# The small early load of wqkv entries: 64 entries over all 640 rows in place of 16 over the first 128

## The chip, the cores and the metric

The kernel runs on one core of one Trainium2 chip. The metric is the device time of one execution in microseconds (us), taken as the median over runs. Before the change it is 274.14 us, the median of 6 runs from 273.8 to 274.5.

## What is computed

The inputs are bf16: x is 2048 x 640 (S x D), wqkv 640 x 1920, wo 640 x 640, w_gate and w_up 640 x 1728, w_down 1728 x 640, gate_w 640 long. With H = 32 heads of 20:

```
def _A_ref(x, wqkv, wo):
    qkv = (x @ wqkv).reshape(B, S, 3, H, Dh) ...            # q, k, v
    phi = lambda t: jnp.where(t > 0, t + 1, jnp.exp(t)) + 1e-6
    pq, pk = phi(q), phi(k)
    kv = einsum("bhsd,bhse->bhde", pk, v);  z = sum of pk over s
    o = (pq @ kv) / (pq . z + 1e-6)
    return o @ wo                                           # heads joined again
def _B_ref(x, w_gate, w_up, w_down):
    return (gelu(x @ w_gate) * (x @ w_up)) @ w_down
g = sigmoid((A_x * gate_w).sum(-1, keepdims=True))
out = g * _A_ref(A_x, A_wqkv, A_wo) + (1 - g) * _B_ref(A_x, B_w_gate, B_w_up, B_w_down)
```

The columns 0 to 639 of wqkv give q, 640 to 1279 give k, 1280 to 1919 give v. One row of wqkv is 3840 bytes in DRAM.

## The kernel before

The program is a plan: `P.op(engine, function, reads, writes)` appends an instruction to its engine's list, and works out from the named reads and writes which semaphores it waits for. At the end the lists are emitted in the order in which they were written. Each engine (TensorE as PE, VectorE as DVE, ScalarE as ACT, GpSimd as POOL, SyncE as SP) runs its own list in order. A load given to "sp" or "act" is issued by that engine's queue, and each has its own semaphore. The 16 DMA engines of the core serve both queues.

The work goes in stages: K and Q projections with phi (a start for tiles 0 and 1, then `KQ(i)` at L540 for tiles 2 to 15), the product of pk and x (`MM`, L597), the feed-forward matmuls (`G`, L701) with the attention's small products between them, and the output tiles (`O_tile`, L865).

The change is in the start. There the loads are written out by hand:

- ACT's queue: first the early load of L357 into `touch`, 16 columns at the end of the SBUF pool, which nothing reads and whose semaphore nobody waits for. Then x tile 1, wk chunks 2 and 4, gate_w, and wq rows 256 to 639 (`load_wq(2, KC, "act")`).
- SP's queue: x tile 0, wk chunks 0, 1 and 3, wq rows 0 to 255 (`load_wq(0, 2)`). Then the DMA transposes of x tiles 2 to 15 (L375), the first of which waits for wk chunk 4.

All but the early load and the transposes are issued at L340. A chunk k is 128 rows of wqkv, `A_wqkv[k * 128:(k + 1) * 128, ...]`, one row per SBUF partition; `load_wk` takes columns 640 to 1279 of it and `load_wq` columns 0 to 639.

PE's list at the start: matmuls on constants (`warm`, L419), transposes of x tile 0 (`T`, L433), more `warm`, the first K matmul of tile 0, the transposes of tile 1, then the K matmuls (`KM`, L453 and L454) of both tiles over chunks 0, 1, 3, then 2 and 4, with the small `gate_col` (L498) between. Then come the Q matmuls (`QM`, L468 and L469), tile 0 and tile 1 in turn over chunks 0, 1, 2, then 3 and 4. The first four need wq chunks 0 and 1, which come by SP's load; the fifth is the first to need the load on ACT's queue. After these `KQ(2)` needs the transposed x tile 2.

The early load reads four numbers of a row, from column 640 on. Before the change these are rows 0, 8, 16, ..., 120, one to each of partitions 0 to 15.

Of the kernel before, what the change touches and what calls it, by code (L numbers as in the profile page):

```python
# [161 lines left out]
def bass_gated_mix__linear_attn_block__geglu_ffn__prompt_kernel(  # L162
# [63 lines left out]
    with (  # L226
# [8 lines left out]
        with contextlib.ExitStack() as stack:  # L235
            dma_sems = [stack.enter_context(nc.semaphore("s_in%d" % i)) for i in range(n_dma_in)]

            P = _Plan(["pe", "act", "dve", "pool", "sp"])
# [9 lines left out]
            def new_dma_key():  # L248
                k = "in%d" % dma_next[0]
                dma_next[0] += 1  # L250
                return k

            def v16(o, n):
                return pool[:, o:o + n]
# [46 lines left out]
            touch = v16(O_TOUCH, 16)  # L301
# [49 lines left out]
            def load_wq(k0, k1, eng="sp"):  # L351
# [2 lines left out]
                       r_wq[k0:k1], eng=eng)  # L354


            P.op("act", lambda e: e.dma_start(touch[0:16, 0:4], A_wqkv[0:128:8, 640:644]),  # L357
                 writes=[P.res("touch")], dma=new_dma_key())
            load_x(0)
            load_wk(0)  # L360
# [569 lines left out]
```

## Time and profile before

| | before |
|---|---|
| median of 6 runs | 274.14 us (273.8 to 274.5) |
| profiled execution, its own time | 274.5 us |
| its span, first to last instruction | 273.3 us |
| mean granted TensorE clock | 1.000 |
| busy, PE / DVE / ACT / POOL | 269.6 / 141.9 / 75.9 / 30.0 us |
| moved by DMA | 23.61 MB, mean 86 GB/s |

How to read the lines below: times are us from the span's start unless marked ns. A group's line has source line, engine, operation, output and input, and a count. In the chain of work each line is a start, a duration, and an engine or transfer; "SPq" is SP issuing a DMA, "issue" is time in which the engine waited for nothing that the profile shows. In the waits, "A <- B: total, times, longest" says that A stood still until B. In the view of one source line, the three durations in ns are the shortest, the median and the longest, and then first and last start. In the list of DMA issues the last number is the median us from issue to landing.

### The profile page before, as it was taken

The numbers are of one execution on the slowest core, as the hardware profiler recorded it, in microseconds if no ns is written. First come the engines' busy times: TensorE is split into PE (matmuls) and PEld (weight loads), VectorE is DVE, ScalarE is ACT, GpSimd is POOL, SyncE is SP. The second block draws the span as 40 slices with busy tenths as digits, with TensorE's granted clock in tenths as the row PEclk, the third lists the DMA queues.
The fourth block names the chain that finished last, engine by engine and source line by source line (L and its number), as shares of the span: only waits on it lengthen the run. The fifth ranks groups of instructions, "written<-read, shape, count | busy, mean of one in ns | idle before, by whom it ended". The sixth has DMA issues, their size and how long they took to land.

```text
span 273.3 us, 3449 instructions
## 1 busy us (share of the span) xinstructions
PE 269.6 (99%) x1369; PEld 128.5 (47%) x1369; DVE 141.9 (52%) x251; ACT 75.9 (28%) x132; POOL 30.0 (11%) x28
## 2 busy tenths in 40 slices
PE   8899999999999999999999999999999999999997
PEld 4455555544445444444444444444444444444444
DVE  2588989998234324999999999634210000000200
ACT  2355555300421454223222223224011121121021
POOL 5000000002240001242433422000000000000000
PEclk9999999999999999999999999999999999999999
DMA  6976999600300011522221211263031110110211
GB/s 210 190 103 124 317 401 388 147 3 9 67 19 2 22 49 51 181 46 48 27 48 24 48 41 35 60 216 108 5 77 38 41 38 19 38 41 19 58 58 41
DMA packets 42160, 23.61 MB, mean 86 GB/s; under 512 B 31519, under 2 KB 40735, under 8 KB 42015
## 3 DMA queue, kind: packets, MB, share of 16 engines
q1 hardware_dynamic: 41269, 22.40, 30.5%
q10 hardware_dynamic: 874, 0.98, 1.0%
q8 instruction: 11, 0.18, 0.3%
q14 instruction: 6, 0.05, 0.1%
HBM read 13.83 MB, written 2.63 MB: 60 GB/s over the span
## 4 chain that ended last, share of the span: by engine, by line
PE 96%; DMA 2%; SPq 1%; issue 0%; DVE 0%
PE ps L701 41%; PE ps L865 23%; PE ps L540 14%; PE ps L597 6%; PE ps L844 4%; DMA pool<-in_A_wqkv_dram 2%; PE ps L812 2%; PE ps L679 2%; PE ps L600 1%; PE ps L468 1%; PE ps L825 1%; SPq L340 1%; PE ps L722 1%; PE ps L740 0%; PE ps L469 0%; PE ps L607 0%
## 5 line engine op out<-in xcount | busy, mean ns | idle before, releaser
L701 PE MATMUL ps<-pool 128*128 128x512 bf16 x520 | 113.7, 379 | 0.0
L701 PEld LDWEIGHTS ps<-pool 128*128 128x128 bf16 x520 | 50.5, 98 | 60.0
L865 PE MATMUL ps<-pool 128*128 128x512 bf16 (+2 forms) x306 | 62.7, 367 | 0.0
L707 ACT ACTIVATE pool<-ps 128x512 f32<-128x512 f32 x52 | 31.0, 597 | 73.1 <-PE ps L701 73.1
L709 DVE TENSOR_TENSOR pool<-ps,pool 128x512 bf16<-128x512 f32 x52 | 34.6, 688 | 31.7 <-PE ps L701 30.4
L865 PEld LDWEIGHTS ps<-pool 128*128 128x128 bf16 x306 | 29.2, 98 | 33.5 <-issue 0.4
L540 PE MATMUL ps<-pool 128*128 128x512 bf16 (+1 forms) x210 | 38.1, 344 | 0.0
L848 DVE TENSOR_TENSOR pool<-ps,pool 128x512 bf16<-128x512 f32 x4 | 2.8, 692 | 61.5 <-PE ps L844 61.5
L755 POOL TENSOR_TENSOR pool<-pool 128x640 f32<-128x640 bf16 x16 | 22.4, 1405 | 73.0 <-DVE pool L757 66.1
L872 ACT ACTIVATE pool<-ps,pool 128x512 bf16<-128x512 f32 (+1 forms) x16 | 10.9, 680 | 68.6 <-PE ps L865 68.6
L540 PEld LDWEIGHTS ps<-pool 128*128 128x128 bf16 x210 | 20.5, 98 | 17.5
L559 DVE SCALAR_TENSOR_TENSOR pool<-ps,pool 128x128 bf16<-128x128 f32 (+2 forms) x42 | 25.3, 602 | 2.4
L550 ACT ACTIVATE pool<-ps 128x640 bf16<-128x640 f32 x28 | 19.7, 703 | 18.2 <-DVE pool L559 10.9
L597 PE MATMUL ps<-pool 128*128 128x512 bf16 x78 | 19.4, 379 | 0.0
L765 DVE TENSOR_TENSOR pool<-pool 128x640 bf16<-128x640 bf16 x16 | 13.2, 825 | 0.6
L763 DVE TENSOR_SCALAR pool<-pool 128x32 f32<-128x32 f32 x16 | 12.8, 802 | 0.6
L757 DVE TENSOR_REDUCE pool<-pool 128x32 f32<-128x640 f32 x16 | 12.9, 808 | 0.0
L645 DVE TENSOR_TENSOR pool<-pool 128x640 f32<-128x640 f32 x14 | 11.6, 826 | 0.5
L844 PE MATMUL ps<-pool 128*128 128x512 bf16 x52 | 11.6, 379 | 0.0
L647 POOL PARTITION_ALL_REDUCE pool<-pool x1 | 4.0, 3971 | 61.6 <-DVE pool L645 61.6
L597 PEld LDWEIGHTS ps<-pool 128*128 128x128 bf16 x78 | 6.9, 98 | 7.3
L556 DVE TENSOR_SCALAR pool<-pool 128x640 bf16<-128x640 bf16 x28 | 9.2, 327 | 1.7 <-ACT pool L550 0.3
(70 smaller groups left out, 105.8 us busy)
## 6 DMA issues: line engine op xcount, KB each, us to landing
out_dram<-pool SPq DMA_DIRECT2D x19, 128.0 KB, 1.7
pool<-in_B_w_gate_dram SPq DMA_DIRECT2D x1, 2080.0 KB, 13.8
pool<-in_B_w_up_dram SPq DMA_DIRECT2D x1, 2080.0 KB, 19.0
pool<-in_A_x_dram SPq DMA_DIRECT2D x1, 1280.0 KB, 9.1
pool<-in_B_w_down_dram SPq DMA_DIRECT2D x1, 1120.0 KB, 6.1
pool<-omg_row SPq DMA_DIRECT2D x1, 1024.0 KB, 4.5
pool<-in_A_x_dram SPq DMA_DIRECT2D x1, 960.0 KB, 6.2
pool<-in_A_wo_dram SPq DMA_DIRECT2D x6, 160.0 KB, 9.8
```

The source lines that it names most:

```text
L540: last = e.matmul(ps[:, b + p, 0:c1 - c0], xT[:, k, i * 128:(i + 1) * 128], wkq[:, k, c0:c1], start=(k == 0), stop=(k == KC - 1))
L550: P.op("act", lambda e: e.activation(e_buf[m], ps_flat[:, o:o + 640], ACT.Exp), reads=banks, writes=[r_e[m]])
L559: P.op("dve", lambda e, c0=c0, c1=c1: e.scalar_tensor_tensor(dst[:, c0:c1], ps_flat[:, o + c0:o + c1], 1.0 + EPS, e_buf[m][:, c0:c1], ALU. ...
L597: last = e.matmul(ps[:, b, :], pk[i][:, c * 128:(c + 1) * 128], x_aug[:, i, 0:512], start=(i == 0), stop=(i == NT - 1))
L701: last = e.matmul(ps[:, b, :], w[:, k, fc * 128:(fc + 1) * 128], xT[:, k, j * 512:(j + 1) * 512], start=(k == 0), stop=(k == KC - 1))
L707: P.op("act", lambda e: e.activation(ge[n], ps[:, gb, :], ACT.Gelu_apprx_tanh), reads=[bank[gb]], writes=[r_ge[n]])
L709: P.op("dve", lambda e: e.tensor_tensor(hT[fc][:, j * 512:(j + 1) * 512], ps[:, ub, :], ge[n], ALU.mult), reads=[bank[ub], r_ge[n]], write ...
L755: P.op("pool", lambda e: e.tensor_tensor(tmp[n], pq[i], z_b, ALU.mult), reads=[r_pq[i], r_zb], writes=[r_tmp[n]])
L757: P.op("dve", lambda e: e.tensor_reduce(den[n], tmp[n].rearrange("p (h d) -> p h d", h=32), AX.X, ALU.add), reads=[r_tmp[n]], writes=[r_de ...
L765: P.op("dve", lambda e: e.tensor_tensor(pq[i].rearrange("p (h d) -> p h d", h=32), pq[i].rearrange("p (h d) -> p h d", h=32), den[n].unsqu ...
L844: last = e.matmul(ps[:, b, :], wd[:, fc, 512:640], hT[fc][:, j * 512:(j + 1) * 512], start=False, stop=(fc == NFC - 2), skip_group_check=True)
L865: last = e.matmul(ps[:, pb, 0:c1 - c0], lhs, rhs, start=False, stop=(q == len(rows) - 1), skip_group_check=True)
```

## The change

The early load takes four numbers each from 64 rows, 0, 10, 20, ..., 630, that is from the whole height of wqkv, and puts them into partitions 0 to 63. It stays at its place at the head of ACT's queue, and everything else is as it was.

```diff
-            P.op("act", lambda e: e.dma_start(touch[0:16, 0:4], A_wqkv[0:128:8, 640:644]),
+            P.op("act", lambda e: e.dma_start(touch[0:64, 0:4], A_wqkv[0:640:10, 640:644]),
                  writes=[P.res("touch")], dma=new_dma_key())
```

## The prediction

> **What bounds the kernel now.** I read the page's first part, then the chain that ended last, then TensorE's own waits.
>
> ```profile
> PE 269.6 (99%) x1369; PEld 128.5 (47%) x1369; DVE 141.9 (52%) x251; ACT 75.9 (28%) x132; POOL 30.0 (11%) x28
> ```
>
> TensorE (PE) is busy 269.6 of 273.3 us, so a change moves the time only through the 3.7 us in which it is not. Its busy time cut into five stretches says where these lie:
>
> ```profile
> 0.00:0.83 0.83, 0.00 (x1) 1.00 0.00 0
> 0.83:3.03 2.20, 2.20 (x7) 1.00 0.44 109
> 3.03:8.77 5.74, 4.85 (x42) 1.00 1.07 317
> 8.77:271.40 262.63, 262.58 (x1323) 1.00 0.30 82
> 271.40:273.30 1.90, 0.00 (x0) 1.00 0.24 69
> ```
>
> The columns are the stretch, its length, PE's busy time (with its instructions), the granted clock, the share of DMA time and GB/s. From 8.77 us on PE stands still for 0.05 us in 262 us, and the granted clock is 1.00 throughout. Nothing that the early load does can be felt after 8.77 us unless a transfer that is now early becomes late. Before that, 0.83 us are start, and 0.89 us idle lie between 3.03 and 8.77. The chain of work, in order of time, tells what ends the last of these waits:
>
> ```profile
> 2.18 0.43 SPq L340
> 2.61 0.04 issue
> 2.65 5.98 DMA pool<-in_A_wqkv_dram
> 8.63 0.14 issue
> 8.77 0.38 PE ps L468
> ```
>
> SP's fifth load, wq rows 0 to 255, is issued at 2.65 us and lands at 8.63; PE's first Q matmul (L468) starts at 8.77. TensorE's waits over the whole run:
>
> ```profile
> PE ps L419 <- PEq L915: 0.8, 1, 0.8
> PE ps L468 <- DMA pool<-in_A_wqkv_dram: 0.8, 1, 0.8
> ```
>
> So the landing of that load sets the end one for one: later by d is slower by d; earlier by d is faster by d until the 0.79 us wait (its length in the timeline) is used up. The K matmuls before it wait for weights once, 0.19 us, so the most that faster early loads can bring is about 0.98 us (0.36%).
>
> **The change part by part.** The early load goes first on ACT's queue:
>
> ```profile
> L357 ACTq DMA_DIRECT2D pool<-in_A_wqkv_dram x1: 416/416/416, 0.8 to 0.8; - x1
> ```
>
> This is its line in the view of that source line, and the same view names nobody under "who waited for it". The removed load has 16 entries of four bf16 numbers (8 bytes), the added one 64: on 16 DMA engines, spread evenly, one entry each before and four each after. No instruction is added, no wait, no other byte moves; the target columns in SBUF have no reader. Four things may still cost.
>
> Issue: 0.416 us for 16 entries, against 0.403 for x tile 0 and 0.407 for wk chunk 0, which have 128 rows each. The issue time does not grow with entries, so I take 0. If it did grow, the activation queue's next issue at 1.23 us would be late by that much, in front of the slack counted below.
>
> Transfer: the landings bound the price of an entry.
>
> ```profile
> pool<-in_A_x_dram SPq DMA_DIRECT2D x1, 160.0 KB, 2.2
> pool<-in_A_x_dram ACTq DMA_DIRECT2D x1, 160.0 KB, 3.3
> pool<-in_A_wqkv_dram ACTq DMA_DIRECT2D x1, 0.1 KB, 2.0
> omg_row<-pool SPq DMA_DIRECT2D x1, 8.0 KB, 10.8
> ```
>
> The last column is us from issue to landing. x tile 0 has 128 entries of 1280 bytes, eight on each engine, and lands 0.2 us later than the early load with its one: 0.2/7 = 0.029 us for each further entry of an engine, payload included. At three further entries that is 0.09 us. The far end is the store of omg, 2048 entries of four bytes, 128 on each engine: (10.8 - 2.0)/127 = 0.069 us for each, or 0.21 us for three. That one writes DRAM, and ours reads DRAM into SBUF as x does, so I take x's row: 0.1 us. Nothing here gives a gain, since no byte is taken away; one could only come from the rows touched (first rival).
>
> One rule of the Trainium skill speaks against the change. The page "DMA: Bandwidth & Descriptors", section "Bandwidth", gives 0.67 us as the floor of a 4 KB load, named as 64 packets at about 10.5 ns each, and calls small transfers dominated by their descriptors. By that figure, an estimate from the page, 48 more packets would be 0.50 us, and the time 274.64. The row of x tile 0 disagrees: 112 more entries than the early load, and 160 KB, for 0.2 us more.
>
> Who pays the 0.1 us: the 16 engines serve SP's queue too, so x tile 0 (landed at 0.79 + 2.2 = 2.99 us, when PE starts on it at 3.03) may be late by 0.1, and PE with it; the waits of 0.19 and 0.79 us behind it would absorb that. What is not absorbed is wq's landing, if all loads in the engines shift alike: +0.1 us at the end. If the other loads fill the holes (the engines move 166 GB/s from 2.5 to 3.0 us, against 371 from 4.5 to 5.0), it is 0. I take +0.05, between 0 and 0.1.
>
> Order on ACT's queue: behind the early load stand x tile 1, wk chunks 2 and 4, gate_w and wq rows 256 to 639. What each can be late by: x tile 1 lands at 1.23 + 3.3 = 4.53, used at 4.77 (L433), with the 0.98 us of waits behind it, so 1.2 us. wq's second part lands at 3.29 + 6.1 = 9.39 and is first used by the fifth Q matmul (L468) at 9.86: 0.47 us. Chunk 4 also releases SP's transposes at 6.33; a transpose lands in some 3.5 us, 9.8, and PE needs the first at 11.49: 1.7 us. The tightest is 0.47 us, and 0.1 us fits in.
>
> The sum is made against the profiled execution: 274.5 us, span 273.3 and 1.2 around it, which becomes 274.55. The median of the six runs is 274.14, 0.36 below that execution, and I keep the shift: 274.14 + 0.05, so **274.2 us**. A measurement of this kernel can tell about 0.2%, 0.55 us, from no change: same means 273.6 to 274.7. Its own range, from no cost and the loads falling better by a few tenths (the two queues share engines, and their order shifts) to 0.21 us plus as much, is 273.7 to 274.6.
>
> **Rival one: priming.** A first read of distant rows of wqkv might cost time, and 64 rows over the whole matrix would pay it ahead of the loads. The rates in half-microsecond windows are where it would show:
>
> ```profile
> 2.50:3.00 0.50, 0.50 (x3) 0.13 (x1) 0.00 (x0) 0.49 (x1) 0.50 (x1) 1.00 0.90 166
> 4.50:5.00 0.50, 0.50 (x7) 0.38 (x8) 0.00 (x0) 0.00 (x0) 0.20 (x1) 1.00 1.08 371
> 5.50:6.00 0.50, 0.50 (x5) 0.31 (x4) 0.17 (x1) 0.00 (x0) 0.00 (x0) 1.00 1.10 254
> 6.00:6.50 0.50, 0.50 (x6) 0.24 (x4) 0.00 (x0) 0.00 (x0) 0.00 (x0) 1.00 0.76 215
> ```
>
> The last column is GB/s. For it: there are two dips while wqkv is loaded. If they ran at 371 GB/s, 0.5 x (1 - 166/371) = 0.28 us would be saved in the first, and 0.16 + 0.21 = 0.37 in the other two, 0.65 in all: below the 0.98 us that PE can use, so 274.14 - 0.65 = 273.5. Against it: the second dip lies on wq's start, whose rows wk's loads have read already; the first, on wk chunk 0, whose rows the load of before touches; while rows 128 on, never touched, come at 371 GB/s. And w_gate, untouched by anything, starts at 388 GB/s in the window from 34 to 35 us. Half of it, 0.3 us, would count as same.
>
> **Rival two: slower, the four reads go one after the other.** Each engine's four entries lie ten rows (38 KB) apart, and no row of the trace shows small entries read so. If an engine finished each before the next, ACT's queue would stand. The price of one: x tile 1 lands 1.1 us later after its issue than x tile 0, having the early load ahead of it, but also tile 0's and wk's packets; I give the early load half, 0.55 us. Three more are 1.65 us, less the 0.47 us of wq's second part: +1.2, so 275.3. It decides past 0.47/3 = 0.16 us an entry, and shows as slower past (0.47 + 0.55)/3 = 0.34. Its bound is the full flight of one entry, from the end of issue at 1.20 to 2.78, 1.58 us: 3 x 1.58 - 0.47 = 4.3, so 278.4. Against it stands x tile 0, whose eight entries overlap, though these are neighbours in memory.
>
> **How the numbers follow.** Forecast, no difference: 0.46, since x's row prices the entries and nobody waits for them. Slower 0.32, as the row for spread reads is missing and a delay of wq's landing has no cover; faster 0.22, as two dips exist but stand at the wrong places. The range 273.4 to 275.3 takes in the priming case's 273.5 and the serial case's 275.3; what it leaves out is the far ends of both, together under 2 in 10.
>
> **What would show it.** Right: the early load still lands some 2.0 to 2.2 us after issue, x tile 1 at about 3.3 to 3.4, and PE's wait at L468 stays within 0.2 us of 0.79 with the first Q matmul near 8.8. Priming: the dips at 2.5 and 5.5 to 6.5 us shallower, and the first Q matmul at 8.2 or before. Serial reads: a landing of the early load over 3 us, and a new wait of PE at the fifth Q matmul. I would be wrong in kind if PE idled after 12 us, for then a transfer that I called covered is not.

## The result, and the profile after

The changed kernel has a median of 274.90 us over 33 runs (274.28 to 277.42), and the kernel before 274.42 us over 74 runs (273.80 to 275.41), more than the six known at the prediction. The ratio is 1.0023, 95% interval 1.0015 to 1.0031: slower by 0.63 us (0.41 to 0.85). The means lie 0.64 us apart, the medians 0.48. The interval excludes no change, and holds the 0.2% up to which I had said "same". Not every execution is slower: 10 of the 33 took 274.51 us or less (49 of 74 before), but 16 took 275.0 or more (4 of 74 before). The profiled execution took 274.67 us (span 273.4), 0.17 more than the one of before, so it is one of the milder ones.

The change's own line in the profile after:

```profile
L357 ACTq DMA_DIRECT2D pool<-in_A_wqkv_dram x1: 541/541/541, 0.8 to 0.8; - x1
```

The issue takes 0.541 us, not 0.416. TensorE's waits over the whole run are others than before:

```profile
PE ps L419 <- PEq L915: 0.8, 1, 0.8
PE ps L433 <- DMA pool<-in_A_x_dram: 0.4, 1, 0.4
PE ps L498 <- DMA pool<-in_gate_w_dram: 0.2, 1, 0.2
```

The wait for wq at L468 has gone. PE stands instead for x tile 1 (L433) and for gate_w (L498). The weight load for x tile 1 starts at 5.47 us after 1.03 us idle; the matmuls before it fill part of that, so that PE itself is idle for 0.45. In the timelines the five transposes of x tile 1 stand so, before:

```profile
4.77 0.44 PE L433 MATMUL ps<-pool 128*128 128x128 bf16 x5
```

and after:

```profile
5.47 0.52 PE L433 MATMUL ps<-pool 128*128 128x128 bf16 x5 [0.45 <-DMA pool<-in_A_x_dram]
```

The chain of work, in order of time, shows the new order:

```profile
0.80 0.54 ACTq L357
1.34 0.04 issue
1.37 0.59 ACTq L340
...
2.00 0.45 ACT L366
...
2.48 0.45 ACTq L340
...
2.97 4.82 DMA pool<-in_gate_w_dram
7.79 0.05 issue
7.84 0.18 PE ps L498
```

It runs through ACT's list now: the early load, x tile 1, an activation that stands between the loads (L366), a wk load, gate_w, which lands at 7.79. (Three dots stand for lines left out.) Before, it ran through SP's queue to wq at 8.63. In the list of DMA issues (last column: us from issue to landing) x tile 0, x tile 1 and the early load stand so:

```profile
pool<-in_A_x_dram SPq DMA_DIRECT2D x1, 160.0 KB, 2.3
pool<-in_A_x_dram ACTq DMA_DIRECT2D x1, 160.0 KB, 4.1
pool<-in_A_wqkv_dram ACTq DMA_DIRECT2D x1, 0.5 KB, 2.5
```

x tile 1 is issued 0.14 us later (1.37 against 1.23), its issue takes 0.59 us in place of 0.45, and it lands at 5.47 instead of 4.53: 0.94 us later. The rates in half-microsecond windows (last column, GB/s; PE's busy time alone) say what lies between. The kernel before:

```profile
2.50:3.00 0.50, 0.50 (x3) 1.00 0.90 166
3.00:3.50 0.50, 0.50 (x7) 1.00 0.93 305
3.50:4.00 0.50, 0.50 (x8) 1.00 0.92 292
```

The kernel after:

```profile
2.50:3.00 0.50, 0.50 (x3) 1.00 1.00 339
3.00:3.50 0.50, 0.50 (x6) 1.00 0.67 113
3.50:4.00 0.50, 0.50 (x8) 1.00 0.71 138
```

The first dip has moved from 2.5 us to 3 us and become longer; in these 1.5 us the engines moved 295 KB after against 382 KB before (0.5 us times the three rates). wk chunk 0 on SP's queue lands earlier, 2.3 us after issue and not 3.1, and x tile 1 on ACT's queue later. From 5.5 to 6.5 us, where before had its second dip, after moves 387 and 361 GB/s, and wq's first part lands at 2.65 + 5.2 = 7.85 us, earlier than before.

All of the difference lies in the start. In the chain the matmuls of `KQ` (L540) begin at 11.66 us before and at 11.85 after, and the rest of the execution, 274.50 - 11.66 = 262.84 and 274.67 - 11.85 = 262.82 us, is the same. I use this marker below: in all 14 profiles of this case the rest is 262.81 to 262.91 us.

### The profile page after: what moved, and what is told of

The parts are those of the page before. It is cut to its first block, busy times and chain, and to the rows that moved or that the text cites. A ratio compares the mean times of both kernels' runs of the same rounds, so it can differ in the third digit from the quotient of the medians.

```text
span 273.4 us, 3449 instructions
## 1 busy us (share of the span) xinstructions
PE 270.0 (99%) x1369; PEld 128.6 (47%) x1369; DVE 142.0 (52%) x251; ACT 75.9 (28%) x132; POOL 30.0 (11%) x28
## 4 chain that ended last, share of the span: by engine, by line
PE 96%; DMA 2%; ACTq 1%; ACT 0%; DVE 0%; issue 0%
PE ps L701 41%; PE ps L865 23%; PE ps L540 14%; PE ps L597 6%; PE ps L844 4%; DMA pool<-in_gate_w_dram 2%; PE ps L812 2%; PE ps L679 2%; PE ps L600 1%; PE ps L468 1%; PE ps L825 1%; PE ps L722 1%; PE ps L740 0%; ACTq L340 0%; PE ps L453 0%; PE ps L469 0%
## 5 line engine op out<-in xcount | busy, mean ns | idle before, releaser
L540 PE MATMUL ps<-pool 128*128 128x512 bf16 (+1 forms) x210 | 38.1, 344 | 0.0
L540 PEld LDWEIGHTS ps<-pool 128*128 128x128 bf16 x210 | 20.5, 98 | 17.5
```

The source lines that it names most:

```text
L540: last = e.matmul(ps[:, b + p, 0:c1 - c0], xT[:, k, i * 128:(i + 1) * 128], wkq[:, k, c0:c1], start=(k == 0), stop=(k == KC - 1))
```

## The experiments

Two theories stood at the outset: it is the number of entries on ACT's queue, or it is the reading of rows far apart. The ratios are to the kernel before on the same chip. The third column is from the one profiled execution of each kernel. The diffs below are cut to the arguments that differ, and e5's loops are put on one line each.

| | early load | x tile 1 issued at, us | ratio (95%) |
|---|---|---|---|
| e4 | none | 0.79 | 1.0025 (1.0007 to 1.0043) |
| e3 | 16 entries over 640 rows | 1.23 | 1.0003 (0.9995 to 1.0012) |
| e6 | 16 entries of 32 bytes | 1.23 | 0.9991 (0.9979 to 1.0004) |
| e8 | 16 entries of w_down | 1.23 | 1.0003 (0.9994 to 1.0012) |
| e10 | 32 entries over 640 rows | 1.23 | 1.0006 (0.9997 to 1.0015) |
| e1 | 64, the changed kernel again | 1.37 | 1.0026 (1.0013 to 1.0039) |
| e2 | 64 over the first 128 rows | 1.38 | 1.0042 (1.0021 to 1.0064) |
| e7 | 64, four to a partition | 1.50 | 1.0033 (1.0012 to 1.0053) |
| e9 | 16, then one more load of 1 | 1.80 | 1.0028 (1.0013 to 1.0044) |

Read by its third column the table is in order: the time of before wherever x tile 1 is issued at 1.23 us, and 0.25 to 0.42% more wherever it is earlier or later. The cost does not grow with the lateness: 0.26 and 0.42% at 1.37 and 1.38 us, 0.28% at 1.80.

**The changed kernel again (e1).**

> The changed kernel again, as the measure for the others on the same chip. Every theory: 1.0015 to 1.0031 of before (about +0.6 us), with x tile 1 landing some 4 us after its issue and TensorE idle before its transposes (L433), as in the profile after.

1.0026, as expected. Its profiled execution took 275.41 us with `KQ` starting at 12.58: the rest, 262.83 us, is again the same, so the executions differ from one another, too, by how the start goes.

**Count or spread (e2, e3).**

```diff
-  touch[0:64, 0:4], A_wqkv[0:640:10, 640:644]
+  touch[0:64, 0:4], A_wqkv[0:128:2, 640:644]      # e2
+  touch[0:16, 0:4], A_wqkv[0:640:40, 640:644]     # e3
```

> 64 entries, but from rows 0, 2, ..., 126. Theory count (the 48 further entries cost on ACT's queue: a longer issue, 0.54 in place of 0.42 us, the next one 0.59 in place of 0.45, and x tile 1 late behind them): as the changed kernel, +0.4 to +0.7 us. Theory spread (reads of far-off rows are what costs): as before, within 0.2 us, and issue and landing of x tile 1 as before (0.45 and 3.3 us).

> 16 entries, but from rows 0, 40, ..., 600. Theory count: as before, within 0.2 us, issue 0.42 us. Theory spread: slower by +0.3 to +0.7 us, with the stall of the loads between 3 and 4 us that the profile after shows.

Count holds, spread falls. e2 has an issue of 0.54 us and then 0.59, x tile 1 lands 4.2 us after issue, and it is slower; e3 has 0.41, 0.45 and 3.3, and is the kernel before in time. The rate from 3 to 4 us is 305 and 287 GB/s in e3.

**No early load (e4).**

> The early load is left out altogether, nothing else; x tile 1 is then first on ACT's queue. Theory count: 0.3 us or more gained on ACT's queue (its issues move ahead by 0.45 us), so same as before or faster by up to 0.5 us, since entries only cost. Theory priming (the early reads of wqkv save time of the later ones): slower than before by 0.3 us or more, with wk chunk 0 landing later than the 3.1 us of before.

Slower by 0.25%, so the count theory's "same or faster" missed: the early load is worth something. The signs of priming are there, slower and wk chunk 0 landing 3.6 us after issue, not 3.1, so this run alone doesn't decide against it; e8 below does. The profile shows another reason. Now x tile 1 and x tile 0 are issued at the same moment, and x tile 0, on which TensorE starts, lands later:

```profile
pool<-in_A_x_dram SPq DMA_DIRECT2D x1, 160.0 KB, 2.7
```

2.7 us in place of 2.2; TensorE's first transposes begin at 3.57 us, not 3.03. wq's first part, on which the chain ends in this kernel too, lands at 8.93 us (before 8.63), and `KQ` starts at 11.95. Two queues' loads share the engines, which is what the Trainium skill states ("DMA: Bandwidth & Descriptors", section "Issuing engines are not separate DMA queues"). It adds that issuing from several engines saves only the issue time, usually small beside the transfer; here ACT's issues moved ahead by 0.44 us (x tile 1 from 1.23 to 0.79), and with them x tile 0 came later and the kernel lost 0.25%.

**Another tensor (e8), and the same bytes in fewer entries (e6).**

```diff
+  touch[0:16, 0:4], B_w_down[0:128:8, 0:4]         # e8
+  touch[0:16, 0:16], A_wqkv[0:128:8, 640:656]      # e6
```

> 16 entries from w_down in place of wqkv; w_down is not loaded until 176 us. Theory spacer (the early load helps only by holding ACT's queue back, so that x tile 0 has the engines to itself; without it x tile 0 landed at 2.7 in place of 2.2 us): as before, within 0.2 us, x tile 0 landing in 2.2 us. Rival priming (reading wqkv early helps wqkv's loads): as without the early load, +0.5 us or more, wk chunk 0 landing later than the 3.1 us of before.

> 16 entries of 32 bytes from rows 0, 8, ..., 120: the 512 bytes of the changed kernel in the number of entries of before. Theory count: as before within 0.2 us, issue 0.42 us. Rival bytes (the payload costs): +0.5 us as the changed kernel.

Both as the kernel before in their ratios. Reading wqkv early has no part in what the early load is worth: sixteen entries of a tensor that is needed at 176 us do as well, with x tile 0 in 2.2 us. And 512 bytes cost nothing as 16 entries. e8's profiled execution is the slowest of its twelve, though, 275.03 us: with ACT's queue on time TensorE stood 0.8 us for wk chunk 1, chunk 3 landed at 7.59 us, and `KQ` began at 12.19, later than in the changed kernel's first profile. So a late queue is not the only thing that makes a start long, and one profile is one execution.

**Entries or partitions (e7).**

```diff
+  touch[0:16, 0:16].rearrange("p (a b) -> p a b", a=4),
+  A_wqkv[0:640:10, 640:644].rearrange("(p a) b -> p a b", a=4)
```

> The same 64 entries from rows 0, 10, ..., 630, but to 16 partitions, four entries in each. Theory count by entries: as the changed kernel, +0.4 to +0.7 us, issue 0.54 us and the next one 0.59. Rival partitions (the longer issue goes with the 64 partitions, not the entries): issue 0.42 us and the time of before.

Slower, so it goes with the entries and not with 64 partitions. The issue was even longer than expected, 0.68 us, and then 0.59.

**Half the step (e10).**

> 32 entries from rows 0, 20, ..., 620. If the cost goes with the entries, 16/48 of the changed kernel's +0.6 us: +0.2 us, and an issue of about 0.46 us. If it goes with a threshold in what x tile 1 can be late by (about 0.2 us before TensorE reaches it), the time of before, with the wait at L433 still near 0.

The time can't tell the two apart: 1.0006 (0.9997 to 1.0015) holds both no change and +0.2 us (1.0007). What failed is the issue that the proportion asked for. It does not grow at all:

```profile
L357 ACTq DMA_DIRECT2D pool<-in_A_wqkv_dram x1: 415/415/415, 0.8 to 0.8; - x1
```

x tile 1 goes out at 1.23 us and lands in 3.2 us, and `KQ` starts at 11.53. So x tile 1 wasn't late, and how late it can be was not put to the test.

**The shift without the entries (e9).**

```diff
   P.op("act", lambda e: e.dma_start(touch[0:16, 0:4], A_wqkv[0:128:8, 640:644]), ...)
+  P.op("act", lambda e: e.dma_start(touch[0:1, 8:12], A_wqkv[0:1, 640:644]), ...)
```

> The early load of before (16 entries), and behind it on ACT's queue one more load of a single entry: ACT's later loads are issued some 0.4 us later with 17 entries in place of 64. At the kernel's end SP also waits for it. Theory late issue (what costs is that ACT's queue is issued 0.29 us later in the changed kernel, x tile 1 first): x tile 1 issued at about 1.65 us, and slower by +0.5 us or more, with TensorE idle before x tile 1 (L433) for 1 us. Rival entries (the 48 further entries slow the engines themselves): as before within 0.2 us, or slower by the shift alone where x tile 1 is still in time.

This run makes ACT's queue late with few entries. ACT's queue, from the timeline:

```profile
1.23 0.54 ACTq L359 DMA_DIRECT2D pool<-in_A_wqkv_dram  x1
1.80 0.36 ACTq L340 DMA_DIRECT2D pool<-in_A_x_dram  x1
```

With 17 entries in place of 64 and a later queue it is slower by 0.28%, and TensorE's waits are those of the changed kernel, two lines further down in the code:

```profile
PE ps L435 <- DMA pool<-in_A_x_dram: 0.5, 1, 0.5
PE ps L500 <- DMA pool<-in_gate_w_dram: 0.3, 1, 0.3
```

The weight load for x tile 1 had stood 1.03 us (TensorE itself 0.45, not the 1 us expected), the dip is there (126 GB/s from 3.0 to 3.5 us), and `KQ` starts at 11.84, as in the changed kernel's first profile (11.85). So a later ACT queue is enough for this cost; 64 entries need not be there. It is not a copy of the changed kernel's shift: x tile 1 goes out 0.57 us later than before, not 0.14, and behind a second load. Whether 0.14 us would cost as much alone, or the 48 further entries add to it in the engines, no run separates.

**gate_w's wait taken away (e5).** gate_w is the load on the chain, and PE's small matmul on it stands in front of K matmuls that don't need it.

```diff
-  for k in (1, 3): KM(0, [k]); KM(1, [k])
-  gate_col()
-  for k in (2, 4): KM(0, [k]); KM(1, [k])
+  for k in (1, 3, 2): KM(0, [k]); KM(1, [k])
+  gate_col()
+  for k in (4,): KM(0, [k]); KM(1, [k])
```

> The changed kernel, with PE's small gate matmul (L498) put behind the K matmuls of chunk 2, about 1.1 us later in PE's order. Theory gate (gate_w, late behind the others on ACT's queue, stands in front of PE's K matmuls of chunks 2 and 4 and is the wait that ends last; 0.23, 0.6 and 0.3 us of PE's waits in three profiles): PE's wait at L498 goes, and 0.2 to 0.5 us of the changed kernel's +0.6 us come back, so +0.1 to +0.4 us. Rival x1 (the wait for x tile 1 alone is what costs): no change, +0.6 us.

1.0026 (1.0007 to 1.0044): nothing that can be told from the changed kernel came back. The wait went, and another took its place, for wk chunk 3 on SP's queue; from the waits and from the chain:

```profile
PE ps L453 <- DMA pool<-in_A_wqkv_dram: 1.2, 1, 1.2
```

```profile
2.18 5.87 DMA pool<-in_A_wqkv_dram
```

In this execution chunk 3 landed at 8.05 us, having been issued at 2.18 as ever. The load that ends last changes from execution to execution (chunk 3 was late in e8, too, with ACT's queue on time), and here it didn't help to shield one of them.

**x tile 1 on SP's queue (e11, e12).** A try at a kernel that beats both.

```diff
   load_x(0)
+  load_x(1)
   load_wk(0)
-  load_x(1, "act")
-  load_wk(1)
+  load_wk(1, "act")
   load_wk(3)
```

> The changed kernel with x tile 1 and wk chunk 1 changed over: x tile 1 second on SP's queue, wk chunk 1 on ACT's behind the early load. Theory x tile 1 (it is late behind the 64 entries, and TensorE's list stands still for it): its wait of 0.9 to 1.4 us at L433 goes, and the time comes to within 0.2 us of before. Rival holes (the loads as a whole run with holes from 3 to 4 us, at 113 to 241 GB/s, so that the bytes arrive late in whatever order): still +0.4 us or more, with TensorE waiting for weights (L453, L468) in place of x.

> The early load of before, with the same change-over. If x tile 1 from ACT's queue costs anything in the kernel before: faster by up to 0.3 us, else the same, since its chain ends in wq's landing. If wk chunk 0, now third on SP's queue and issued 0.45 us later, sets TensorE's first K matmul (4.46 us before): slower by up to 0.4 us at that point, of which the later wait for wq covers all.

1.0066 (1.0049 to 1.0084) and 1.0075 (1.0050 to 1.0100), slower than either kernel. x's wait went, but wk chunk 0, issued at 1.71 us, took 4.4 us in e11 and 4.2 in e12, and PE stood for it; e12's waits:

```profile
PE ps L453 <- DMA pool<-in_A_wqkv_dram: 1.6, 1, 1.6
```

In e12 the first K matmul starts at 6.00 us in place of 4.50, 1.50 later and not the 0.4 I had allowed. `KQ` starts at 12.17 in place of 11.66, so 0.99 us were won back, about the 0.98 of waits that the prediction had counted: the cover held, but the lateness was too large for it.

In e11 `KQ` starts at 13.76 us, 1.59 after e12's, though its first K matmul starts at 6.29, only 0.29 later, and TensorE waits for no load after that. There the matmuls themselves take longer, up to 9.1 us. Two K matmuls from e11's timeline:

```profile
8.70 0.62 PE L453 MATMUL ps<-pool 128*128 128x512 bf16 x1
9.21 0.38 PE L453 MATMUL ps<-pool 128*128 128x512 bf16 x1
```

and the first of e12's:

```profile
6.00 0.38 PE L453 MATMUL ps<-pool 128*128 128x512 bf16 x1 [1.62 <-DMA pool<-in_A_wqkv_dram]
```

The same instruction takes 0.6 us early on and 0.38 later, and the change comes at another time in each execution. In the kernel before, the first K matmul, at 4.50 us, takes 0.38 already; in the changed kernel the first, at 4.28, takes 0.63, and in e7 so does the one at 6.09. The clock column of the windows reads 1.00 in these stretches all the same. What sets the time of the change, and whether it comes later more often in the slower kernels, no run here tests. It is a rival for part of their cost.

So the swap does not single out x tile 1, as it was meant to; it makes another early load late. The signs of the rival with the holes came in e11 (TensorE waits at L453, and the engines move 156 and 177 GB/s from 3 to 4 us), but e12, with 333 and 264 GB/s there, is as slow by its ratio.

## Why the prediction was right or wrong

The measured 274.90 us lies inside the range of 273.4 to 275.3, but above the 273.7 to 274.6 of the forecast's own case. Part of this is the measure: the kernel before was 274.42 us in the longer series, 0.28 above the median I started from. The other part, 0.48 us between the two long series (0.63 by the ratio) where I had +0.05, is the change. That the range held it is due to its width, which was there for rival two; the sum did not give it. Of the signs named for being right none came: the early load lands after 2.5 us and not 2.0 to 2.2, x tile 1 after 4.1 and not 3.3 to 3.4, and PE's wait at L468 is gone. Two things held. The priming rival fell: rows never touched cost nothing more (e3), and another tensor does as well (e8). And behind the start nothing moved (262.84 and 262.82 us).

**The step that failed first is the issue.** I took 0 because 128 rows issue in 0.40 us. The 64 small entries take 0.541 in place of 0.416, and the next issue on the queue 0.593 in place of 0.448: ACT's queue was late by 0.125 + 0.145 = 0.27 us (2.06 against 1.78 at the third issue). I had said what lateness would face, but priced it at none.

**The step that failed with more weight is the slack.** By my counts 0.27 us fits under the tightest slack, 0.47 us, and x tile 1's 1.2 us. This took a load issued later by d as landing later by d. x tile 1 landed 0.94 us later for an issue 0.14 us later, 0.28 at its end. That the dip of the engines lay on it fits the rates, but is argued, not shown. Even 0.94 is less than the 1.2 us that I gave it: TensorE began its transposes 0.70 us later (5.47 against 4.77) and `KQ` only 0.19 later, so 0.51 was won back. What stood against the rest is gate_w: TensorE waited 0.23 us for it, more than the 0.19. gate_w I had listed on ACT's queue without counting its slack. e5 shows that its wait alone isn't the root either, as chunk 3 stood in its place.

**wq's landing does not set the end one for one.** It landed 0.78 us earlier (7.85 against 8.63) and the kernel was slower. I had counted with this load alone; in the profiles here the chain ends its waits in wq, in gate_w, or in wk chunk 0 or 3.

**The transfer term** was 0.09 to 0.21 us by the rows. The early load's landing went from 2.0 to 2.5 us, of which 0.125 is issue. The 0.50 us for 48 more packets, estimated from the page, is nearer to this than x tile 0's row, and the sum by it, 274.64, is nearer the result. That the entries' own time is what costs is not shown by that: e9 pays as much with 17 entries on a later queue.

**Rival two** named the right queue and the wrong cause. Of its signs, a landing of the early load past 3 us is in no profile here. A wait at the fifth Q matmul is in e7's alone, where its weight load stood 0.23 us. e2 is slower without rows far apart, and e9 without 64 entries.

**The clock.** I read 1.00 throughout from the column of the windows. The matmuls of the kernel before say otherwise for the start: those of 128 columns take 0.31 us up to 4.1 us and 0.22 from 4.7 on. The sum did not use it, but it is a second thing that makes starts differ, as e11 shows.

Four things stay open. Why the rate falls to 113 to 138 GB/s for a microsecond when ACT's queue is late was seen in each of the slower kernels with a late queue (from 113 to 259 GB/s in the windows from 3 to 4 us) but not taken apart; that the loads of the two queues then begin together is an inference. And which of ACT's four later loads matters most wasn't settled, as the swap that should have told it moved the wait to wk chunk 0. Nor was it settled what the 48 entries cost apart from the later issues, and how much of the +0.63 us is matmuls that run slowly for longer; the executions of 275 us and more were mostly not profiled.

## What to carry to other kernels

A load that nobody reads can still hold a queue back, and so order what two queues send to the same engines; before changing it, look at when the next load behind it is issued, not at its bytes. Slack counted from issue times is not safe where the transfers share engines: a shift of 0.14 us in an issue went with 0.94 us in a landing. When several loads land close to the need, taking away the wait on one may only bring up the next, as in e5. And before a start is put down to a late load, look at how long the matmuls themselves take.

## What was not expected of the hardware

The issue time of a load on ACT's queue is not set by its rows or bytes alone: 16 and 32 entries of 8 bytes take 0.416 and 0.415 us, 128 rows of 1280 bytes 0.39 to 0.45, but 64 entries of 8 bytes 0.541 on 64 partitions and 0.680 on 16; a single entry, issued second (e9), took 0.54. Behind the loads of 64 entries the next issue took 0.59. gate_w's issue, the same load in every run, takes 0.57 to 0.58 us, but 0.37 in e9, so the time is not the load's own alone.

A 128x512 matmul took 0.6 us in the first microseconds and 0.38 afterwards, and the change came before 4.5 us in the kernel before and after 8.7 in e11.
